# Column tiles for the remainders of a mixture-of-experts kernel's second products, and a smaller descriptor area

## The chip, the cores and the metric

The kernel runs on one core of a Trainium2 chip. The metric is the device time of one execution in microseconds (us), the median of the runs. Lower is better.

## The reference

Attention with a decay over 8 batches of 8 heads, 576 positions and 64 values per head gives 4608 rows of 512 features. Each row goes to the one expert of 8 that has its largest gate logit.

```python
for e in range(E):                      # E = 8, D = 512, F = 1024, N = 4608
    mask = e_idx == e
    h = np.maximum(x[mask] @ w1[e], 0.0)
    ye = h @ w2[e]
    out[mask] = gate_w[mask, None] * eom[mask, e, None] * ye
```

`gate_w` is the softmax weight of the chosen expert, `eom` a sigmoid gate. `h @ w2[e]` is the second product, which the change touches.

## The kernel before

The first part, up to about 356 us, is attention, with the routing of the rows beside it. The second part computes the experts one after the other. Experts 0 and 1 come first with 640 rows each; the other six are ranked by their counts and get the capacities of `CAPS`: 640, 608, 592, 576, 560 and 512 rows. Rows beyond an expert's capacity would go through a loop at the end (`tc.For_i`, line 1255 for the end of a block and line 1323 for the end of the program), which makes no turn with these inputs.

For each expert the rows are gathered from a buffer in DRAM by indirect DMAs on POOL's queue (line 808), 128 at a time, and turned by DMA transposes on SP's queue (`gather_turn`, line 814) into `xT`.

The first products (`up_products`, line 1057) go over 8 chunks `fc` of the hidden features. For each chunk and each of 4 parts of the contraction there are three products (upper by upper, upper by lower and lower by upper half of the operands' split into two 16-bit numbers). The moving operand is `xT`, 512 rows and then the rest of the capacity, and the result stands in `hp` (two buffers for each column piece). ACT takes the positive part into `hh` (line 1066), DVE the remainder of that rounding into `hl` (line 1067); `split_w2` splits the expert's second weights in between, on DVE and POOL in turns (line 1001).

The second products (`down_sum`, lines 1079 to 1085) go over row tiles of 128 rows. A tile is one sum in PSUM: for each of the 8 chunks three matmuls, whose stationary operand is `hh` or `hl` (128 features by 128 rows) and whose moving operand is a chunk of `w2`, 512 columns wide. A capacity that is no multiple of 128 gets a whole last tile; its superfluous rows have indices beyond the output and are not written. `y`, the sum, has two buffers.

After each tile `down_out` (line 1093) evicts `y` on ACT with the row's weight as scale into `ys` (three buffers), and POOL scatters the 128 rows to the output by an indirect DMA (line 1094). In between, the next expert's first weights are split on ACT and POOL (`load_w1`, lines 776 and 777), two chunks after each of the first four tiles.

The order on each engine is that of the code (`manual_schedule`). On PE the sums of an expert's tiles follow each other, and the next expert's first products follow the last tile.

[...]

Of the kernel before, what the change touches and what calls it, by code (L numbers as in the profile page):

```python
# [9 lines left out]
F32 = mybir.dt.float32  # L10
# [5 lines left out]
ALU = mybir.AluOpType  # L16
# [4 lines left out]
P = 128  # L21
B, H, S, D = 8, 8, 576, 64
NT = B * S
DM = H * D
# [48 lines left out]
def attn_moe(tc, *args, **kw):  # L73
    with ExitStack() as ctx:
        _attn_moe(ctx, tc, *args, **kw)


def _attn_moe(ctx, tc, qk, vm, f, wg, w1, w2, out):
    nc = tc.nc
# [685 lines left out]
    NF = FF // P  # L765
    ND = DM // P

    def fetch_w1(pool, we, fc, bufs):
        raw = pool.tile([P, ND, P], F32, name="w1r", bufs=bufs)
        nc.sync.dma_start(raw, we[fc])  # L770
        return raw
# [17 lines left out]
    W2, W2r = [], {}  # L789
# [13 lines left out]
    def rows_x(pool, ids=None):  # L803
        return (pool.tile([P, CT, 2], I32, name="ids") if ids is None else ids,
                pool.tile([P, CT, 2, 2, DM // P // 2, P], F16, name="xT", bufs=1))

    def gather_rows(x, t, known=NT):
        nc.gpsimd.indirect_dma_start(
            out=xg[:, t], out_offset=None, in_=xbuf[0:known],
            in_offset=bass.IndirectOffsetOnAxis(ap=x[0][:, t, 0:1], axis=0),  # L810
            bounds_check=known - 1, oob_is_err=False)

    def gather_turn(x, t):
        nc.sync.dma_start_transpose(x[1][:, t].rearrange("p h j k n -> p (h j k) n"), xg[:, t])
# [174 lines left out]
    m2 = ctx.enter_context(tc.tile_pool(name="m2", bufs=2, reuse_waits="tile"))  # L989
    m1 = ctx.enter_context(tc.tile_pool(name="m1", bufs=1, reuse_waits="tile"))  # L990
    pm = ctx.enter_context(tc.tile_pool(name="pm", bufs=2, space=PSUM, reuse_waits="tile"))
    def fetch_w2(we, fc):
        raw = m2.tile([P, DM], F32, name="w2r", bufs=6)
        nc.sync.dma_start(raw, we[fc])
        return raw

    def split_w2(raw, eng):
        h = m2.tile([P, DM], F16, name="w2h", bufs=8)
        l = m2.tile([P, DM], BF16, name="w2l", bufs=8)
        nc.scalar.copy(out=h, in_=raw)  # L1000
        eng.tensor_tensor(l, raw, h, op=ALU.subtract)  # L1001
        return h, l
# [42 lines left out]
    def hidden():  # L1045
        return m1.tile([P, NF, CAP], F16, name="hh"), m1.tile([P, NF, CAP], F16, name="hl")

    def up_products(w1s, x, cols, fc):
        xT = x[1]
        wh, wl = w1s[fc]  # L1050
        hp = [pm.tile([P, 512], F32, name=f"hp{j}", bufs=2) for j in range(len(cols))]
        for k in range(ND):
            for i, (w, j) in enumerate(((wh, 0), (wh, 1), (wl, 0))):
                for m, (c0, c1) in zip(hp, cols):
                    t0, t1 = c0 // P, c1 // P
                    x = xT[:, t0:t1, k // 2, j, k % 2] if c1 % P == 0 else xT[:, t0, k // 2, j, k % 2, 0:c1 - c0]
                    nc.tensor.matmul(m[:, 0:c1 - c0], w[:, k], x,  # L1057
                                     start=k == 0 and i == 0, stop=k == ND - 1 and i == 2)
        return hp

    def up_split(hp, h, cols, fc):
        hh, hl = h
        for m, (c0, c1) in zip(hp, cols):
            sl = slice(c0, c1)
            m = m[:, 0:c1 - c0]
            nc.scalar.activation(out=hh[:, fc, sl], in_=m, func=AF.Relu)  # L1066
            nc.vector.scalar_tensor_tensor(hl[:, fc, sl], m, 0.0, hh[:, fc, sl],  # L1067
                                           op0=ALU.max, op1=ALU.subtract)

    def up(w1s, x, cols, h=None):  # L1070

        h = h or hidden()
        for fc in range(NF):
            up_split(up_products(w1s, x, cols, fc), h, cols, fc)
        return h

    def down_sum(w2s, h, t):
        hh, hl = h
        y = pm.tile([P, DM], F32, name="y", bufs=2)
        sl = slice(t * P, (t + 1) * P)  # L1080
        for fc in range(NF):
            wh, wl = w2s[fc]
            nc.tensor.matmul(y, hh[:, fc, sl], wh, start=fc == 0, stop=False)  # L1083
            nc.tensor.matmul(y, hh[:, fc, sl], wl, start=False, stop=False)  # L1084
            nc.tensor.matmul(y, hl[:, fc, sl], wh, start=False, stop=fc == NF - 1)  # L1085
        return y
# [3 lines left out]
    def down_out(x, y, t, looped=False):  # L1090
        ids = x[0]
        ys = m2.tile([P, DM], F32, name="ys", bufs=3)
        nc.scalar.activation(out=ys, in_=y, func=AF.Copy, scale=ids[:, t, 1:2].bitcast(F32))  # L1093
        ins = nc.gpsimd.indirect_dma_start(  # L1094
            out=out, out_offset=bass.IndirectOffsetOnAxis(ap=ids[:, t, 0:1], axis=0),
            in_=ys, in_offset=None, bounds_check=NT - 1, oob_is_err=False)
        if not looped:
            for other in written:
                tc.declare_no_dep(ins.ins, other.ins, reason="distinct rows")
            written.append(ins)  # L1100

    def down(w2s, x, h, t0, t1, looped=False):
        for t in range(t0, t1):
            down_out(x, down_sum(w2s, h, t), t, looped)

    def weights(load, we):
        return [load(we, fc) for fc in range(NF)]

    def load_w1(we, fc, raws=None, eng=nc.gpsimd):
        return split_w1(m2, raws[fc] if raws else fetch_w1(m2, we, fc, 8), 8, eng)  # L1110


    x = st["early"]

    with tc.manual_schedule(engines=ENGINES):
# [15 lines left out]
        h = hidden()  # L1131
# [27 lines left out]

        first_splits(0, 4)  # L1160
        down_out(x, down_sum(W2, h, 0), 0)
        for t in range(CT):
            gather_rows(x1, t)
# [6 lines left out]
        W1, W2, x = W1n, [], x1  # L1170
# [20 lines left out]
        ids = m1.tile([P, R, CT, 2], I32, name="idsr")  # L1191
# [12 lines left out]
        def pieces(cap):  # L1204

            return [(0, SM)] + ([(SM, cap)] if cap > SM else [])

        def expert(r):

            cap = CAPS[r]  # L1210
            ei = nc.values_load(rank[0:1, r:r + 1], engines=[mybir.EngineType.SP], min_val=0, max_val=E - 1)
            return dict(cap=cap, ids=ids[:, r],
                        w1=w1[bass.ds(ei, 1)].rearrange("a f p k n -> (a f) p k n"),
                        w2=w2[bass.ds(ei, 1)].rearrange("a f p n -> (a f) p n"))

        e = dict(cap=CAP, w2=w2[1])
        for n in range(len(CAPS) + 1):
            cap = e["cap"]
            cols = pieces(cap) if n else [(0, EARLY), (EARLY, CAP)]
            tiles = -(-cap // P)  # L1220
            nx = expert(n) if n < len(CAPS) else None
            nt = -(-nx["cap"] // P) if nx else 0
            for fc in range(NF):
                up_split(up_products(W1, x, cols, fc), h, cols, fc)
                W2.append(split_w2(W2r[fc], nc.gpsimd if fc % 2 else nc.vector))
                if fc + AHEAD < NF:
                    W2r.append(fetch_w2(e["w2"], fc + AHEAD))
                if nx:
                    if fc == 0:
                        x1 = rows_x(m2, nx["ids"])  # L1230
                    if 2 <= fc < 2 + nt:
                        gather_rows(x1, fc - 2)
                    if fc >= NF - AHEAD:
                        W1r = (W1r if fc > NF - AHEAD else []) + [fetch_w1(m2, nx["w1"], fc - NF + AHEAD, 8)]
            W1n, W2n = [], []
            for t in range(nt):
                gather_turn(x1, t)
            for t in range(tiles):
                y = down_sum(W2, h, t)
                if nx:  # L1240
                    for fc in range(2 * t, min(2 * t + 2, NF)):
                        W1n.append(load_w1(nx["w1"], fc, W1r))
                        if fc + AHEAD < NF:
                            W1r.append(fetch_w1(m2, nx["w1"], fc + AHEAD, 8))
                    if t == 3:
                        W2r = [fetch_w2(nx["w2"], fc) for fc in range(AHEAD)]
                down_out(x, y, t)
                if n == 0 and t == 3:
                    ncum = overflow_slots()
                if n == 2 and t == 0:  # L1250
                    nsl = nc.values_load(ncum, min_val=0, max_val=(NT - min(CAPS)) // P + E)
            if nx:
                e, x, W1, W2 = nx, x1, W1n, W2n

    with tc.For_i(0, nsl, 1) as i:
# [7 lines left out]
        n = pr.tile([P, 512], F32, name="ms", bufs=1)  # L1263
# [8 lines left out]
        x = rows_x(m2)  # L1272
# [7 lines left out]
        h = up(weights(load_w1, w1[bass.ds(ei, 1)].rearrange("a f p k n -> (a f) p k n")), x, [(0, P)])  # L1280
# [46 lines left out]
```

## Time and profile before

| | |
|---|---|
| median of 3 runs | 752.74 us (752.64 to 755.38) |
| profiled execution | 751.45 us, its span 749.8 us |
| PE busy | 721.5 us (96%), 8819 matmuls |
| POOL busy | 456.9 us (61%) |
| DVE, ACT busy | 357.5 us (48%), 339.8 us (45%) |
| mean granted TensorE clock | 0.994 of full speed |

The span runs from the first to the last instruction of the profiled execution. An engine's busy time counts its computing instructions and POOL's DMA instructions; semaphores, branches and drains are not counted. Ends of matmuls are modelled, so the time of one is read from the distance of the starts. `L1084` is line 1084, and `out<-in` names the tiles that an instruction writes and reads.

### The profile page before, as it was taken

Reading aid. Unit: us, or ns where it says so; the run is one execution under the profiler, and the core shown is the slowest. Engines: PE = TensorE matmul, PEld = TensorE weight load, DVE = VectorE, ACT = ScalarE, POOL = GpSimd, SP = SyncE. Lnnn points to the kernel's source line nnn. Section 1 sums busy time; section 2 is a strip of 40 time slices with the busy share of each in tenths; the row PEclk is TensorE's granted clock in tenths of the full one; section 3 lists DMA queues with packets and bytes.
Section 4 is the critical chain, followed back from the end, with each engine's and each line's share of the span. In section 5 each row is a group of like instructions: output and inputs, shape, how many; then the busy total and the mean of one; then the engine's idle time right before and its main releaser. Section 6 shows DMA issues by size and latency. Waiting matters only on the chain. (4 is left out here: it accounts for less than half of the span.)

```text
span 749.8 us, 21552 instructions
## 1 busy us (share of the span) xinstructions
PE 721.5 (96%) x8819; PEld 446.8 (60%) x8842; DVE 357.5 (48%) x837; ACT 339.8 (45%) x765; POOL 456.9 (61%) x513
## 2 busy tenths in 40 slices
PE   4999999999999999999999999999999999999993
PEld 2677777777777777776567545445454454444441
DVE  7667687788788887877314133113022031130210
ACT  4456665567666565654323423324324243243320
POOL 9969698898989898862603544534626436345121
PEclk9999999999999999999999999999999999999997
DMA  5445566666777566265744734825836448256100
GB/s 154 156 127 175 160 169 156 162 166 162 186 176 181 150 168 137 59 145 167 193 108 156 162 125 155 244 75 154 235 121 138 179 136 224 82 155 204 47 29 24
DMA packets 119525, 110.67 MB, mean 148 GB/s; under 512 B 82750, under 2 KB 92158, under 8 KB 119424
## 3 DMA queue, kind: packets, MB, share of 16 engines
q1 hardware_dynamic: 108566, 71.50, 36.8%
q10 hardware_dynamic: 4618, 18.88, 8.5%
q0 software_dynamic: 6240, 18.88, 7.9%
q8 instruction: 70, 1.15, 0.6%
q14 instruction: 31, 0.25, 0.1%
HBM read 72.47 MB, written 19.88 MB: 123 GB/s over the span
## 5 line engine op out<-in xcount | busy, mean ns | idle before, releaser
L428 POOL TENSOR_TENSOR plo<-p 128x512 f16<-128x512 f32 x182 | 191.6, 1069 | 34.7 <-ACT p L426 33.3
L1057 PE MATMUL hp<-xT,w1h 128*128 128x512 f16 (+2 forms) x960 | 174.9, 298 | 0.1
L1067 DVE SCALAR_TENSOR_TENSOR hl<-hp,hh 128x512 f16<-128x512 f32 (+2 forms) x120 | 54.2, 485 | 247.0 <-ACT hh L1066 241.5
L426 ACT ACTIVATE p<-sc 128x512 f32<-128x512 f32 x192 | 111.6, 595 | 70.9 <-PE sc L305 64.5
L331 DVE TENSOR_REDUCE nR<-mx 128x2 f32<-128x1024 f32 (+4 forms) x154 | 121.4, 805 | 46.2 <-PE mx L305 44.5
L305 PE MATMUL sc<-qk 64*128 64x448 f32 (+5 forms) x644 | 128.1, 471 | 0.0
L1085 PE MATMUL y<-w2h,hl 128*128 128x512 f16 x312 | 118.2, 379 | 1.2
L1083 PE MATMUL y<-w2h,hh 128*128 128x512 f16 x312 | 118.2, 379 | 0.0
L1057 PE MATMUL hp<-xT,w1l 128*128 128x512 f16 (+2 forms) x480 | 111.8, 298 | 0.0
L1084 PE MATMUL y<-w2l,hh 128*128 128x512 bf16 x289 | 109.5, 379 | 0.0
L1057 PEld LDWEIGHTS <-w1h 128*128 128x128 f16 x960 | 74.6, 98 | 55.6 <-issue 0.2
L1066 ACT ACTIVATE hh<-hp 128x512 f16<-128x512 f32 (+2 forms) x120 | 47.0, 433 | 118.3 <-PE hp L1057 116.6
L1001 POOL TENSOR_TENSOR w2l<-w2r,w2h 128x512 bf16<-128x512 f32 x28 | 32.3, 1153 | 103.1 <-ACT w2h L1000 103.1
L305 PEld LDWEIGHTS <-pick 64*128 64x128 bf16 (+1 forms) x1152 | 58.3, 96 | 48.7 <-issue 26.3
L1094 POOL DMA_INDIRECT out_dram<-ys,idsr x29 | 29.0, 1001 | 72.9 <-ACT ys L1093 68.7
L1093 ACT ACTIVATE ys<-y,idsr 128x512 f32<-128x512 f32 x29 | 19.9, 688 | 104.6 <-issue 60.1
L499 PE MATMUL av<-Vs,p 128*128 128x65 f16 x640 | 66.0, 193 | 1.3 <-ACT xr L546 1.3
L500 PE MATMUL av<-Vs,p 128*128 128x64 bf16 x640 | 65.8, 195 | 0.6 <-issue 0.6
L501 PE MATMUL av<-Vs,plo 128*128 128x65 f16 x640 | 65.5, 192 | 0.0
L305 PE MATMUL mx<-qk 64*128 64x512 bf16 (+3 forms) x372 | 57.3, 301 | 8.3 <-DMA qk<-in_qk_dram 5.5
L500 PEld LDWEIGHTS <-p 128*128 128x128 bf16 x640 | 59.4, 97 | 1.4 <-issue 1.4
L499 PEld LDWEIGHTS <-p 128*128 128x128 bf16 x640 | 59.2, 97 | 1.3
(219 smaller groups left out, 1397.4 us busy)
## 6 DMA issues: line engine op xcount, KB each, us to landing
qk<-in_qk_dram ACTq DMA_DIRECT2D x31, 576.0 KB
w1r<-in_w_dram SPq DMA_DIRECT2D x64, 256.0 KB
w2r<-in_w_dram SPq DMA_DIRECT2D x64, 256.0 KB
v<-in_vm_dram SPq DMA_DIRECT2D x15, 576.0 KB
xbuf<-x SPq DMA_DIRECT2D x16, 512.0 KB
Eq<-mts SPq DMA_DIRECT2D x64, 0.1 KB
xbuf<-x SPq DMA_DIRECT2D x16, 64.0 KB
xT<-x SPq DMA_TRANSPOSE x62
```

Source lines behind the costliest of these rows:

```text
L305: nc.tensor.matmul(dst(i), w(i), x(i), start=start, stop=stop)
L331: nc.vector.tensor_reduce(o, x, axis=AX.X, op=ALU.max, negate=True)
L426: nc.scalar.activation(out=f32, in_=src, func=AF.Exp, scale=0.125)
L428: eng.tensor_tensor(lo, f32, upper(f32), op=ALU.subtract)
L499: nc.tensor.matmul(dst, ph, vv[:, 0:W], start=kc == 0, stop=False)
L500: nc.tensor.matmul(dst[:, 0:D], ph, vv[:, W:].bitcast(BF16), start=False, stop=False)
L501: nc.tensor.matmul(dst, pl, vv[:, 0:W], start=False, stop=kc == qc)
L1057: nc.tensor.matmul(m[:, 0:c1 - c0], w[:, k], x, start=k == 0 and i == 0, stop=k == ND - 1 and i == 2)
L1067: nc.vector.scalar_tensor_tensor(hl[:, fc, sl], m, 0.0, hh[:, fc, sl], op0=ALU.max, op1=ALU.subtract)
L1083: nc.tensor.matmul(y, hh[:, fc, sl], wh, start=fc == 0, stop=False)
L1084: nc.tensor.matmul(y, hh[:, fc, sl], wl, start=False, stop=False)
L1085: nc.tensor.matmul(y, hl[:, fc, sl], wh, start=False, stop=fc == NF - 1)
```

## The change

The last tile of an expert, if it has at most 96 rows, is no longer computed by `down_sum` and `down_out`, but by `down_narrow`. It takes the first 64 rows as a group of column tiles 64 wide and, if there are more, the next 32 as a group of column tiles 32 wide. In a group of `n` rows, `k = 128 / n` matmuls stand beside each other in the array, each with its own chunk of the contraction; their sums come to lie in different partitions of one PSUM bank, and `narrow_out` adds them on DVE with the row's weight: one operation for the first, one for each further. The scatter then covers 64 or 96 rows. The number of matmuls of a group stays 24, each of 512 columns. The descriptor area is 2048 bytes instead of the default.

```diff
+        put_rows(ys, x, t, looped)
+
+    def put_rows(ys, x, t, looped=False):
         ins = nc.gpsimd.indirect_dma_start(
-            out=out, out_offset=bass.IndirectOffsetOnAxis(ap=ids[:, t, 0:1], axis=0),
+            out=out, out_offset=bass.IndirectOffsetOnAxis(ap=x[0][0:ys.shape[0], t, 0:1], axis=0),
             in_=ys, in_offset=None, bounds_check=NT - 1, oob_is_err=False)
...
+    def narrow_sum(w2s, h, r0, n):
+
+        hh, hl = h
+        y = pm.tile([P, DM], F32, name="y", bufs=2)
+        k = P // n
+        for f0 in range(NF // k):
+            for i in range(3):
+                for j in range(k):
+                    fc = j * (NF // k) + f0
+                    nc.tensor.matmul(y[j * n:(j + 1) * n], (hl if i == 2 else hh)[:, fc, r0:r0 + n],
+                                     w2s[fc][i % 2], start=f0 == i == 0, stop=f0 == NF // k - 1 and i == 2)
+        return y
+
+    def narrow_out(x, t, ys, y, n, p0):
+
+        w = x[0][p0:p0 + n, t, 1:2].bitcast(F32)
+        dst = ys[p0:p0 + n]
+        nc.vector.tensor_scalar(dst, y[0:n], w, None, op0=ALU.mult)
+        for j in range(1, P // n):
+            nc.vector.scalar_tensor_tensor(dst, y[j * n:(j + 1) * n], w, dst, op0=ALU.mult, op1=ALU.add)
+
+    def down_narrow(w2s, x, h, t, rest):
+
+        ys = m2.tile([P, DM], F32, name="ys", bufs=3)
+        for p0, n in ((0, 64), (64, 32)):
+            if p0 < rest:
+                y = narrow_sum(w2s, h, t * P + p0, n)
+                narrow_out(x, t, ys, y, n, p0)
+        put_rows(ys[0:64 if rest <= 64 else 96], x, t)
...
             for t in range(tiles):
-                y = down_sum(W2, h, t)
+                rest = cap - t * P
+                y = down_sum(W2, h, t) if rest > 96 else None
...
-                down_out(x, y, t)
+                if y is None:
+                    down_narrow(W2, x, h, t, rest)
+                else:
+                    down_out(x, y, t)
...
-    nc = _bacc.Bacc("TRN2", target_bir_lowering=False, num_devices=1)
+    nc = _bacc.Bacc("TRN2", target_bir_lowering=False, num_devices=1, dynamic_dma_scratch_size=2048)
```

## Rows read from the trace of the kernel before

**Rows 1.** The page's first part: busy time, share of span, instructions.
```profile
PE 721.5 (96%) x8819; PEld 446.8 (60%) x8842; DVE 357.5 (48%) x837; ACT 339.8 (45%) x765; POOL 456.9 (61%) x513
```
**Rows 2.** Stretches: length, busy us (instructions) by engine, granted clock, DMA share, GB/s.
```profile
521.57:547.47 25.90, 25.74 (x119) 11.73 (x121) 0.85 (x2) 8.43 (x15) 14.27 (x13) 1.00 0.73 198
547.47:571.63 24.16, 24.16 (x193) 12.76 (x192) 8.27 (x18) 9.31 (x22) 9.54 (x9) 1.00 0.38 120
571.63:597.53 25.90, 25.74 (x119) 11.77 (x121) 0.84 (x2) 8.12 (x15) 14.27 (x13) 1.00 0.67 196
...
737.60:749.80 12.20, 0.00 (x0) 0.00 (x0) 0.00 (x0) 0.69 (x1) 0.97 (x1) 0.63 0.04 15
```
**Rows 3.** PE in order of time, capacity 608: fifth tile's and next expert's first matmul.
```profile
542.29 0.38 PE L1083 MATMUL y<-w2h,hh 128*128 128x512 f16 x1
...
547.48 0.67 PE L1057 MATMUL hp<-xT,w1h 128*128 128x512 f16 x4
```
**Rows 4.** PE in order of time, attention, 64 rows by 64 columns of the array.
```profile
100.12 0.41 PE L305 MATMUL mx<-qk 64*64 64x512 bf16 x2
100.34 0.40 PE L305 MATMUL mx<-Ek,Eq 63*64 63x512 f16 x2
100.56 0.22 PE L305 MATMUL mx<-qk 64*64 64x64 bf16 x2
100.59 0.22 PE L305 MATMUL mx<-Ek,Eq 63*64 63x64 f16 x2
100.62 0.22 PE L305 MATMUL mx<-negm,pick 64*64 64x64 bf16 x2
100.77 0.54 PE L305 MATMUL sc<-qk 64*128 64x320 f32 x2
```
**Rows 5.** Weight loads in order of time: corners of 64x64, and a full tile.
```profile
100.34 0.14 PEld L305 LDWEIGHTS <-qk 64*64 64x64 bf16 x2
...
547.04 0.10 PEld L1085 LDWEIGHTS <-hl 128*128 128x128 f16 x1
```
**Rows 6.** DVE, ACT and POOL in order of time after that fifth tile; brackets: idle before.
```profile
551.29 0.84 DVE L1067 SCALAR_TENSOR_TENSOR hl<-hp,hh 128x512 f16<-128x512 f32 x2 [28.07 <-ACT hh L1066]
...
547.73 0.69 ACT L1093 ACTIVATE ys<-y,idsr 128x512 f32<-128x512 f32 x1 [4.49 <-PE y L1085]
...
548.69 0.98 POOL L1094 DMA_INDIRECT out_dram<-ys,idsr  x1 [4.18 <-ACT ys L1093]
555.00 1.15 POOL L1001 TENSOR_TENSOR w2l<-w2r,w2h 128x512 bf16<-128x512 f32 x1 [5.33 <-ACT w2h L1000]
```
**Rows 7.** Groups by line and shape: busy us, mean ns, idle before.
```profile
L1067 DVE SCALAR_TENSOR_TENSOR hl<-hp,hh 128x512 f16<-128x512 f32 x48 | 33.2, 692 | 215.9 <-ACT hh L1066 211.3 <-issue 4.5
```
**Rows 8.** Lines 1315 (start), 1323 and 1255 (end): ns min/median/max, first and last start.
```profile
L1315 POOLq INC_SWDGE_SEM  x1: 27/27/27, 0.2 to 0.2; - x1
L1315 POOLq DRAIN  x1: 184/184/184, 0.4 to 0.4; - x1
...
L1323 POOLq EVENT_SEMAPHORE  x4: 17/17/17, 749.0 to 749.6; - x4
L1323 POOLq DRAIN  x3: 40/103/6452, 742.5 to 749.5; - x3
...
L1255 PEldq EVENT_SEMAPHORE  x13: 51/51/51, 737.6 to 742.5; - x13
L1255 POOLq INC_SWDGE_SEM  x1: 1747/1747/1747, 738.7 to 738.7; - x1
```
**Rows 9.** Issues of DMAs by tile: count, median us from issue to landing.
```profile
xg<-xbuf,idsr POOLq DMA_INDIRECT x29, 3.5
out_dram<-ys,idsr POOLq DMA_INDIRECT x29, 2.7
...
xg<-xbuf,ids POOLq DMA_INDIRECT x8, 6.0
...
xg<-xbuf,idsl POOLq DMA_INDIRECT x2, 4.1
```

## The prediction, made before the changed kernel was run

> **What bounds the kernel now.** The first view to read is the page's busy share [rows 1]: PE is busy 96% of the span, every other engine 61% or less. That average says little of one stage, so the next view is the table of stretches [rows 2], cut at the borders between the first products ("up") and the second products ("down") of the ranked experts. In a down stretch of 25.90 us PE is busy 25.74 us, in an up stretch all of 24.16 us, at the full granted clock, while DVE has 0.85 us of work in a down stretch, ACT 8 and POOL 14. The list in order of time shows the same from close by [rows 3]: the fifth row tile of an expert starts at 542.29 us, its successor, the next expert's first product, at 547.48 us, with no idle time noted on either. So in these stages a microsecond taken from PE is a microsecond of the span. The last row of the table [rows 2] shows another kind of stretch: 12.2 us at the end with no matmul at all. What fills it is in the lists by line of the closing instructions [rows 8]: POOL's one long DRAIN of 6.45 us, from 742.5 us on, and after it, from 749.0 us, the last semaphores. All other engines' waits of the loop's end (line 1255) are over by 742.5 us. The page's chain of waits doesn't show this, as it counts no such instruction as work; the drain still stands alone on the path to the end.
>
> **The change, part by part.** *What is removed.* Of the six ranked experts four have a fifth tile with 96, 80, 64 and 48 rows (capacities 608, 592, 576, 560 less 512); those of 640 and 512 rows keep full tiles. Each fifth tile now costs a whole tile: 24 matmuls of 512 columns in 547.48 - 542.29 = 5.19 us [rows 3], 0.216 us apiece. Four make 20.7 us, all on the path.
>
> *What is added on PE.* A remainder is computed in groups of 64 or 32 rows, a group again with 24 matmuls of 512 columns, but in rounds of 2 (64 columns wide) or 4 (32 wide) that lie side by side in the array. A group of 64 has 12 rounds, one of 32 has 6. Remainders 64 and 48 take one group of 64; 96 and 80 take one of 64 and one of 32. That is 4 x 12 + 2 x 6 = 60 rounds. The trace has no column tile that uses all 128 rows. The nearest are the attention's products in 64x64 corners [rows 4]: two matmuls of 512 columns, each in its own rows and columns, start at 100.12 us, the next two at 100.34 us, the following step at 100.56 us. A round costs 0.22 us, not twice 0.216, and its second member lags 0.03 us (0.41 us for the two, where one takes 0.38 in rows 3). The next nearest is the full tile, where matmuls queue at 0.216 us [rows 3]. So a round of two lies between 0.216 us (all at once) and 0.43 us (in turn), one of four between 0.216 and 0.86 us. I take 0.22: the corners too are separate columns of the array with a separate moving operand, and their loads, of 64 columns, are the kind that the change uses [rows 5].
> Loads: a round needs two or four; two take 0.14 us [rows 5], so one takes 0.11 and its partner the same lag of 0.03. In the corners, as in the full tiles, loads run beside matmuls at work, so I count none, but the lag of the members, 0.03 us a group of 64 and 0.09 us a group of 32. If that cover is gone a round has 0.11 us more.
> A change of tile shape: steps of 64 columns in the corners follow each other at 0.03 us (100.56, 100.59, 100.62), and the step after it, with another shape, came 0.15 us later [rows 4], so a change costs 0.12 us. Remainders with one group change twice, those with two groups three times: 10 x 0.12 = 1.2 us.
> Sum: 4 x (12 x 0.22 + 0.03) + 2 x (6 x 0.22 + 0.09) + 1.2 = 10.7 + 2.8 + 1.2 = 14.7 us in place of 20.7: **6.0 us less**. Ends: 60 x 0.216 = 13.0 us with changes at nothing (7.8 less), and 6 groups x 24 x 0.216 + 1.2 = 32.3 us if all wait in turn (11.6 more).
> [...]
>
> *What moves off PE.* The eviction by ACT (0.69 us, starting 0.25 us after the successor has begun [rows 3, 6]) becomes 2 DVE operations for a group of 64 and 4 for one of 32. Their nearest row is the DVE operation of the same width with a PSUM input, 0.69 us [rows 7]. After the last matmul of a remainder 1.4 or 2.8 us of DVE work follow; in the old tile's times it would end near 547.7 + 2.8 = 550.5 us. DVE is free: it idled 28 us before 551.29 us [rows 6]. Were it later, hl would be late, and PE would miss its buffer hp only two steps, some 6 us, after its start. On POOL the scatter of the remainder waits for it, from 548.7 to some 550.7 us, and POOL's next work comes at 555.00 us [rows 6], so nothing stands behind it. The second group needs the y buffer of the fourth tile, which ACT empties within 1 us of that tile's end, 1.8 us before it is asked for. The weights and the gathered rows of the next expert aren't what PE waits for: no idle time stands before its first product [rows 3], and POOL and ACT have some 11 and 17 us to spare in each down stretch [rows 2]; 1 to 3 us less time for them costs nothing. What is late next is again PE.
>
> *The descriptor area.* It is cut from the constructor's default of 16384 bytes to 2048. It takes part in nothing but POOL's 78 indirect DMAs: 29 + 8 + 2 gathers and as many scatters [rows 9]. At the program's start, before any of them, POOL's DRAIN took 0.184 us, and later ones at its end 0.103 and 0.040; the one that follows the 78 took 6.452 us, though the last semaphore of the data was in by 742.5 us [rows 8]. Another POOL instruction that looks after these DMAs went from 0.027 to 1.747 us [rows 8]. I read that as a cost per DMA whose descriptors are still kept: 6.45 / 78 = 0.083 us. No row shows a smaller area, so the ends are 6.45 us (nothing changes) and 0.10 us (nothing kept). If the large area kept all 78, an eighth of it keeps at least 78 / 8, some 10; the rest must have been given back earlier. Estimate: 10 x 0.083 = 0.8 us, **5.6 us less**, all of it at the end where it hides behind nothing. The giving back, 68 x 0.083 us, falls on POOL's DMAs from the tenth on, about 0.8 us per expert against the slack above. A POOL that waits for space meets DMAs ten places back, 25 us or more ago among the experts, that landed after 2.7 to 3.5 us in the median [rows 9]: no wait.
> [...]
>
> **Sum.** 6.0 + 5.6 = 11.6 us less. The profiled execution, 751.45 us with its span of 749.8, would become 739.9 us; it lies 1.3 us under the median of the runs, 752.74 us, from which the forecast is **741.1 us**.
>
> **Rivals.** *The drain doesn't depend on the area* (a fixed price, or one per DMA ever issued): only PE's 6.0 us remain, 746.7 us. For it: no row has another area. Against it: the three short drains and the other instruction's growth.
> *Loads are not covered in column tiles*: a round takes 0.22 + 0.11 us, 60 rounds and the changes 60 x 0.33 + 1.2 = 21.0 us, so nothing is gained on PE; the drain gives 752.7 + 0.3 - 5.6 = 747.4 us.
> *Column tiles run in turn* (the slower side): where two streams through the same 128 rows can't run at once, every narrow matmul takes its 0.216 us, six groups cost 32.3 us, and 752.7 + 11.6 - 5.6 = 758.7 us. The corners don't exclude it, as their rows differ too. It decides from a mean round of (20.7 + 5.6 - 1.2) / 60 = 0.42 us on.
> *Neither part works* (loads uncovered, drain as before): 753 us.
>
> **How the numbers follow.** Forecast 0.60, fixed drain 0.10, loads uncovered 0.12, in turn 0.10, neither 0.05; 0.03 is left for a mixture on the slower side. The forecast's best ends (7.8 and 6.35) give 738.6 us; upwards 747.5 takes in the second and third cases, together 0.82. A measurement can tell about 0.5%, 3.8 us, from no change: faster 0.82 (the first three), same 0.06, slower 0.12.
>
> **What would show it.** After, the four fifth tiles should take 2.9 us (one group) and 4.4 us (two) from their first matmul to the next expert's first, with rounds 0.22 us apart and no idle time on PE behind them; rounds of 0.33 or 0.43 us point to the third and fourth cases. POOL's long DRAIN should be near 1 us, and its DMA instructions still about 1 us. The forecast is wrong if PE idles at the next expert's start for W1, xT or a buffer, or if the drain keeps its 6.45 us.

## The result, and the profile after

| | before | after |
|---|---|---|
| median of 4 runs | 752.69 us (752.23 to 755.38) | 741.84 us (741.30 to 742.90) |
| ratio, 95% interval | | 0.9846 [0.9826, 0.9867] |
| profiled execution, its span | 751.45, 749.8 us | 742.90, 741.2 us |

The change makes the kernel 10.9 us faster, where 11.6 were forecast (741.1 us). The sizes of the two parts are to be read from the stretches and from POOL's closing DRAIN; several terms of the sum were off, and they nearly cancel.

The first part of the page of after answers [rows 1]: PE's busy time fell by 2.9 us only, while DVE took over 12.5 us. The whole kernel's busy time is no measure of the gain here. From the first matmul of the experts' second products on it fell by 6.3 us (379.97 to 373.71); ahead of it, where the change does nothing, it was 3.3 us more (341.54 to 344.88), as after's execution was slower early on (see the last section). The matmuls are more (8871 instead of 8819), as a remainder of two groups has 48 instead of 24.
```profile
PE 718.6 (97%) x8871; PEld 444.3 (60%) x8890; DVE 370.0 (50%) x853; ACT 336.6 (45%) x761; POOL 455.9 (62%) x513
```
Stretches of after, with the columns of [rows 2]: the down stretches of the capacities 608, 592, 576 and 560, and the end without matmuls.
```profile
524.02:548.96 24.94, 24.84 (x145) 11.13 (x145) 2.06 (x4) 8.43 (x15) 14.26 (x13) 1.00 0.77 205
573.13:598.06 24.93, 24.82 (x144) 11.13 (x145) 2.04 (x4) 8.09 (x15) 14.26 (x13) 1.00 0.71 204
621.59:645.12 23.53, 23.42 (x121) 10.59 (x121) 0.82 (x2) 8.21 (x15) 14.25 (x13) 1.00 0.72 205
668.26:691.79 23.53, 23.42 (x121) 10.57 (x121) 0.81 (x2) 8.06 (x15) 14.24 (x13) 1.00 0.63 191
733.40:741.20 7.80, 0.00 (x1) 0.00 (x0) 0.00 (x0) 0.69 (x1) 0.97 (x1) 0.65 0.09 28
```
Each of the four took 25.90 us before. Two fell by 0.96 us (remainders with two groups), two by 2.37 us (one group): 6.7 us in all, where the sum had 6.0. The granted clock is 1.00 in them as before; the only other level on record in the two traces is 0.50, from 740.79 us on in before and from 735.79 us on in after, when the matmuls are over. The end fell from 12.20 to 7.80 us.

PE of after in order of time around the remainder of capacity 608, as [rows 3]; x2 and x4 are matmuls side by side that the view joins.
```profile
544.52 0.38 PE L1085 MATMUL y<-w2h,hl 128*128 128x512 f16 x1
544.84 0.41 PE L1114 MATMUL y<-w2h,hh 128*64 128x512 f16 x2
545.08 0.38 PE L1114 MATMUL y<-w2l,hh 128*64 128x512 bf16 x2
545.29 0.38 PE L1114 MATMUL y<-w2h,hl 128*64 128x512 f16 x2
...
547.23 0.38 PE L1114 MATMUL y<-w2h,hl 128*64 128x512 f16 x2
547.54 0.40 PE L1114 MATMUL y<-w2h,hh 128*32 128x512 f16 x4
547.77 0.39 PE L1114 MATMUL y<-w2l,hh 128*32 128x512 bf16 x4
...
548.63 0.39 PE L1114 MATMUL y<-w2h,hl 128*32 128x512 f16 x4
548.96 0.64 PE L1057 MATMUL hp<-xT,w1h 128*128 128x512 f16 x3
```
From 545.08 to 547.23 us lie 10 rounds of 0.215 us, and from 547.77 to 548.63 us 4 of 0.215 us: two or four matmuls of 512 columns in the time of one, though all of them use the same 128 rows of the array. A change of shape shows as 0.31 us between two starts (547.23 to 547.54), 0.09 us more than a round, and another 0.01 to 0.02 us in the first round after it.

The weight loads of after in order of time, in the same remainder, as [rows 5].
```profile
547.02 0.11 PEld L1114 LDWEIGHTS <-hl 128*64 128x64 f16 x2
547.54 0.12 PEld L1114 LDWEIGHTS <-hh 128*32 128x32 f16 x8 [0.41 <-issue]
547.77 0.11 PEld L1114 LDWEIGHTS <-hl 128*32 128x32 f16 x4
```
The loads of a round take 0.11 us together and lie inside the rounds of 0.215 us.

DVE and POOL of after in order of time behind that remainder, as [rows 6].
```profile
547.72 0.74 DVE L1122 TENSOR_SCALAR ys<-y,idsr 64x512 f32<-64x512 f32 x1 [22.05 <-PE y L1114]
548.50 0.75 DVE L1124 SCALAR_TENSOR_TENSOR ys<-y,idsr,ys 64x512 f32<-64x512 f32 x1
549.28 0.74 DVE L1122 TENSOR_SCALAR ys<-y,idsr 32x512 f32<-32x512 f32 x1
550.06 2.32 DVE L1124 SCALAR_TENSOR_TENSOR ys<-y,idsr,ys 32x512 f32<-32x512 f32 x3
552.78 0.84 DVE L1067 SCALAR_TENSOR_TENSOR hl<-hp,hh 128x512 f16<-128x512 f32 x2 [0.40 <-ACT hh L1066]
```
```profile
552.66 0.94 POOL L1097 DMA_INDIRECT out_dram<-ys,idsr  x1 [5.71 <-DVE ys L1124]
556.49 1.15 POOL L1001 TENSOR_TENSOR w2l<-w2r,w2h 128x512 bf16<-128x512 f32 x1 [2.88 <-ACT w2h L1000]
```
The cover held. hl starts 552.78 - 548.96 = 3.82 us after the next expert's first matmul, as before (551.29 - 547.48 = 3.81 us, [rows 3, 6]), and POOL's next split 7.53 us after it (before: 7.52 us). But DVE had only 0.40 us to spare.

Closing instructions of after by line: minimum, median and longest in ns, first and last start, as [rows 8].
```profile
L1292 PEldq EVENT_SEMAPHORE  x13: 51/51/51, 733.4 to 739.0; - x13
L1292 POOLq INC_SWDGE_SEM  x1: 487/487/487, 734.5 to 734.5; - x1
...
L1360 POOLq DRAIN  x3: 40/103/1307, 739.1 to 740.9; - x3
```
The long DRAIN fell from 6452 to 1307 ns, 5.15 us less (forecast: 5.6). The other instruction, INC_SWDGE_SEM, fell with it, from 1747 to 487 ns.

Last, the way from the last scatter to that DRAIN. After, it took 739.1 - 734.45 = 4.65 us:
```profile
734.45 0.97 POOL L1097 DMA_INDIRECT out_dram<-ys,idsr  x1 [4.26 <-POOLq L1292]
```
and before 742.5 - 738.64 = 3.86 us ([rows 8], and this row of before):
```profile
738.64 0.97 POOL L1094 DMA_INDIRECT out_dram<-ys,idsr  x1 [4.21 <-POOLq L1255]
```
So 0.8 us came back at the end. The sum of the three is -6.68 - 5.15 + 0.8 = -11.0 us, and the medians differ by 10.9. The spans of the two profiled executions differ by 8.55 us only, because after's was 2.3 us behind already at the first matmul of the experts' second products (358.68 us against 356.41), long before the first narrow tile; the last section returns to that.

### The profile page after: what moved, and what is told of

Its sections match the earlier page's. It is cut to its first block, busy times and chain, and to the rows that moved or that the text cites. A ratio compares the mean times of both kernels' runs of the same rounds, so it can differ in the third digit from the quotient of the medians.

```text
span 741.2 us, 21637 instructions
## 1 busy us (share of the span) xinstructions
PE 718.6 (97%) x8871; PEld 444.3 (60%) x8890; DVE 370.0 (50%) x853; ACT 336.6 (45%) x761; POOL 455.9 (62%) x513
## 5 line engine op out<-in xcount | busy, mean ns | idle before, releaser
L1085 PE MATMUL y<-w2h,hl 128*128 128x512 f16 x280 | 106.1, 379 | 1.0
L1083 PE MATMUL y<-w2h,hh 128*128 128x512 f16 x280 | 106.1, 379 | 0.0
L1084 PE MATMUL y<-w2l,hh 128*128 128x512 bf16 x261 | 98.9, 379 | 0.0
L501 PEld LDWEIGHTS <-plo 128*128 128x128 f16 x640 | 59.4, 99 | 0.0
```

What stands on the lines that cost most here:

```text
L501: nc.tensor.matmul(dst, pl, vv[:, 0:W], start=False, stop=kc == qc)
```

## The experiments

### Each part alone

`area_only` is the kernel before with the smaller area.
```diff
-    nc = _bacc.Bacc("TRN2", target_bir_lowering=False, num_devices=1)
+    nc = _bacc.Bacc("TRN2", target_bir_lowering=False, num_devices=1, dynamic_dma_scratch_size=2048)
```


> The kernel before with the small descriptor area alone. Theory (POOL's closing DRAIN costs a fixed 0.18 us and 0.080 us for each indirect DMA whose descriptors are still kept; the line through 6.452 us with 78 kept and 1.307 us after the change gives 14 kept): DRAIN near 1.3 us, the time 5.1 us below before, 747.5 us; POOL's DMA instructions a little longer from the fifteenth on, PE as before. Rival (the DRAIN got shorter because the narrow tiles' scatters are shorter or earlier, not by the area): DRAIN 6.45 us, 752.7 us.

Measured: 748.91 us (748.04 to 751.14) beside 754.97 of before in that session, ratio 0.9922 [0.9896, 0.9947]. Its closing DRAIN, in the list by line:
```profile
L1323 POOLq DRAIN  x3: 40/103/735, 745.8 to 747.1; - x3
```
The price of the DRAIN depends on the area, but 0.735 us is neither the 1.3 us that the theory wanted nor the 1.307 us of the change at the same 2048 bytes. So neither the area nor the 78 DMAs alone set what is kept.

`tiles_only` is the changed kernel with the default area.
```diff
-    nc = _bacc.Bacc("TRN2", target_bir_lowering=False, num_devices=1, dynamic_dma_scratch_size=2048)
+    nc = _bacc.Bacc("TRN2", target_bir_lowering=False, num_devices=1)
```


> The change with the descriptor area left at its default. Theory: the down stretches of the four ranked experts stay at 24.94, 24.94, 23.53 and 23.52 us instead of 25.90, which is 6.7 us together, and the DRAIN is back at 6.4 us: 746.1 us. Rival (the two parts help each other, for example the tiles are only fed in time with POOL relieved): less than 5 us below before, with idle time on PE behind a narrow tile.

Measured: 747.29 us (745.81 to 750.09), ratio 0.9904 [0.9876, 0.9931]. One down stretch, and the closing instructions by line:
```profile
522.34:547.27 24.93, 24.93 (x146) 11.10 (x145) 2.06 (x4) 8.42 (x15) 14.24 (x13) 1.00 0.78 205
```
```profile
L1292 POOLq INC_SWDGE_SEM  x1: 1747/1747/1747, 732.8 to 732.8; - x1
...
L1360 POOLq DRAIN  x3: 40/103/6452, 736.8 to 743.8; - x3
```
The four down stretches are those of the change to 0.01 us, and the DRAIN is that of before. So the area does nothing to the tiles. The tiles do touch the DRAIN, though only where the area is small: it takes 0.735 us without them and 1.307 us with them. By the medians the parts gain 6.1 and 7.7 us, by the rows 5.0 (the DRAIN and the way to it) and 6.4; the intervals, 4.0 to 7.9 and 5.2 to 9.4 us, take that in. The product 0.9922 x 0.9904 = 0.9827 lies at the edge of the interval of the change, so the sum is better read from the rows. The rivals "fixed drain" and "neither" fall, each by its own run.

### Column tiles in turn

`one_by_one` gives PE the same matmuls in another order: all of one column tile, then all of the next.
```diff
-        for f0 in range(NF // k):
-            for i in range(3):
-                for j in range(k):
+        for j in range(k):
+            for f0 in range(NF // k):
+                for i in range(3):
```


> The changed kernel with the loop over the column tiles outermost in a group, so that neighbours in PE's queue belong to the same column tile. Theory (tiles run beside each other only where neighbours in the queue belong to different ones): each of the six groups takes 24 x 0.216 = 5.2 us instead of 2.6 (64 wide) or 1.3 (32 wide), 4 x 2.6 + 2 x 3.9 = 18 us more than the changed kernel, near 760 us, slower than before. Rival (PE picks matmuls of free column tiles out of its queue): 742 us as with the change.

Measured, in a single execution: 751.91 us. The down stretches are 28.02, 28.02, 25.28 and 25.28 us, 9.7 us more than in the change: neither the 18 us of a strict order nor nothing. PE in order of time in the group of 64 rows:
```profile
545.70 0.38 PE L1114 MATMUL y<-w2l,hh 128*64 128x512 bf16 x1
545.92 0.38 PE L1114 MATMUL y<-w2h,hl 128*64 128x512 f16 x1
545.92 0.59 PE L1114 MATMUL y<-w2h,hh 128*64 128x512 f16 x2
546.16 0.56 PE L1114 MATMUL y<-w2l,hh 128*64 128x512 bf16 x2
546.38 0.56 PE L1114 MATMUL y<-w2h,hl 128*64 128x512 f16 x2
546.60 0.38 PE L1114 MATMUL y<-w2h,hh 128*64 128x512 f16 x1
```
Up to 545.92 us one matmul starts every 0.215 us. Then the second column tile's first matmul starts beside the first tile's ninth, while the tenth to twelfth, which stand before it in the program, are still to come; they start in the next three rounds, each beside one of the second tile. The rows don't name the column tile; it follows from the order of the operands, which repeats with each chunk (w2h,hh, then w2l,hh, then w2h,hl). So a tile's end overlaps the next one's beginning by four rounds. That gives 24 - 4 = 20 rounds for a group of 64 (12 in the change) and, with three such borders, 24 - 12 = 12 rounds for one of 32 (6 in the change). A remainder of two groups then has 14 rounds more, 14 x 0.2155 = 3.0 us, and one of one group 8, 1.7 us; measured were 28.02 - 24.94 = 3.08 and 25.28 - 23.53 = 1.75 us. The theory that wanted 18 us, in which matmuls start in the program's order without exception, falls, and so does the one that wanted nothing: PE reaches ahead, but only by three matmuls.

### Only groups of 32

`groups_32` takes the 64 rows of the first group as two groups of 32. The rounds on PE stay as many (6 + 6 instead of 12), DVE gets 8 operations instead of 2 for these rows.
```diff
-        for p0, n in ((0, 64), (64, 32)):
+        for p0, n in ((0, 32), (32, 32), (64, 32)):
```


> The changed kernel with all remainders in groups of 32 rows: two groups for 64 and 48 rows, three for 96 and 80. The rounds on PE stay 60, two changes of tile shape fall away (0.2 us less), and DVE has 8 or 12 operations of 0.69 us per remainder instead of 2 or 6. Theory (PE's cover holds only as far as y's two buffers): the third group waits for the first one's four DVE operations, which end some 1.3 + 2.8 = 4.1 us after the remainder's start where it is asked for after 2.7 us; 1.4 us of idle time on PE in each of the two remainders with three groups, none before the next expert's products: 741.8 + 2.8 - 0.2 = 744.4 us. Rival (DVE is late for the next expert's hl as well): idle time also on PE within the next first products, 2 us or more for each remainder, 750 us or more. Rival (DVE keeps up): 741.6 us.

Measured: 748.03 us (747.25 to 748.72) beside 754.97, ratio 0.9908 [0.9877, 0.9939]. Its stretches say how much of the tiles' gain is gone: the down stretches are 26.95, 26.95, 23.52 and 23.52 us, 4.0 us more than in the change, and the first products behind two of them take 0.7 us more, 4.7 of 6.7 us in all. PE in order of time, at the border of the second and the third group of capacity 608:
```profile
546.84 0.39 PE L1114 MATMUL y<-w2h,hl 128*32 128x512 f16 x4
549.18 0.40 PE L1114 MATMUL y<-w2h,hh 128*32 128x512 f16 x4 [1.95 <-DVE ys L1124]
```
and DVE of that kernel:
```profile
546.05 0.74 DVE L1122 TENSOR_SCALAR ys<-y,idsr 32x512 f32<-32x512 f32 x1 [20.76 <-PE y L1114]
546.82 2.31 DVE L1124 SCALAR_TENSOR_TENSOR ys<-y,idsr,ys 32x512 f32<-32x512 f32 x3
```
PE makes a group of 32 in 1.3 us, DVE empties its y in 3.1 us, and y has two buffers: the third group starts 0.05 us after DVE has left the first. That costs 1.95 us in each of the two remainders with three groups. Where there are only two groups, the down stretch is that of the change (23.52 us), but the DVE work runs on into the next expert, and behind one of them PE waits 0.51 us for hl:
```profile
701.36 0.59 PE L1057 MATMUL hp<-xT,w1h 128*128 128x512 f16 x2 [0.51 <-DVE hl L1067]
```
This wait comes 701.36 - 695.49 = 5.9 us after that expert's first matmul, at the place where the prediction put it (two steps, some 6 us). So the choice of 64 before 32 matters, and it matters on DVE, not on PE. The mechanism was the expected one, the size was not: 1.95 us of idle time in place of 1.4, and the wait for hl of the first rival beside it, though not behind every remainder.

### The size of the area

Five kernels differ from the change in one number, the area: `area_512`, `area_1024`, `area_3072`, `area_4096` and `area_8192`. `change_again` is the change itself once more (2048).
```diff
-    nc = _bacc.Bacc("TRN2", target_bir_lowering=False, num_devices=1, dynamic_dma_scratch_size=2048)
+    nc = _bacc.Bacc("TRN2", target_bir_lowering=False, num_devices=1, dynamic_dma_scratch_size=512)
```
`area_512` and `area_4096` were run first, to see whether the DRAIN goes with the area.

> The changed kernel with an area of 512 bytes, a quarter of the change's. Theory (a fixed 0.18 us and 0.080 us for each DMA kept, 3 or 4 kept): DRAIN near 0.45 us, 0.85 us below the changed kernel, near 741.0 us. Rival (POOL now waits for space, since the DMA three places back was issued only 4 us ago where five gathers follow each other at 1.3 us, and gathers land after 3.5 to 6 us): POOL's DMA instructions or the waits before them grow to several us, gathers come late, and PE idles before an expert's first products: 742 us or more, up to 750.

> The changed kernel with an area of 4096 bytes, twice the change's. Theory (0.18 us and 0.080 us for each DMA kept, twice as many kept, 28): DRAIN near 2.4 us, 1.1 us above the changed kernel, near 742.9 us. Rival (the DRAIN's length has a step, not a slope: short as soon as the area has been used more than once): 1.3 us, 741.8 us. Rival (it counts all DMAs ever issued as soon as the area holds more than a few): 6.45 us, 747 us.

Measured: 741.26 us, ratio 0.9839 [0.9811, 0.9866] and 741.92 us, ratio 0.9838 [0.9813, 0.9864]. Their DRAINs by line, first with 512 bytes, then with 4096:
```profile
L1292 POOLq INC_SWDGE_SEM  x1: 247/247/247, 732.8 to 732.8; - x1
...
L1360 POOLq DRAIN  x3: 40/103/327, 737.2 to 738.3; - x3
```
```profile
L1292 POOLq INC_SWDGE_SEM  x1: 467/467/467, 734.6 to 734.6; - x1
...
L1360 POOLq DRAIN  x3: 40/103/1225, 739.1 to 740.8; - x3
```
A DRAIN that grows with the area would be 2.4 us with 4096 bytes; it is a little shorter than with 2048. That theory, which is also the prediction's (an eighth of the area keeps an eighth of the DMAs), fell. The next one: each DMA whose descriptors are still kept costs 0.0815 us on top of 0.083 us; descriptors are given back only when a new DMA finds no space, and then those of all DMAs but the last seven. What is kept at the end then depends on where in this cycle the last DMA falls, and must be worked out DMA by DMA; where fewer than eight DMAs find room (512 and 1024 bytes), the oldest goes for each new one. Three more areas were run on that theory.

> The changed kernel once more, beside the next ones on the same chip: its DRAIN 1.31 us as before, 0.985 of the kernel before.

> The changed kernel with an area of 1024 bytes. New theory from the five DRAINs seen so far (0.327, 0.735, 1.225, 1.307 and 6.452 us): the DRAIN takes 0.083 us and 0.0815 us for each DMA whose descriptors are still kept, and POOL gives descriptors back only when a new DMA finds no space, then all but the last seven DMAs. At 1024 bytes (half of the 14 DMAs of 2048) seven are kept at any time: DRAIN 0.65 us, 0.65 us below the change. POOL gives one back at each DMA. Rival (each DMA then waits for its seventh predecessor): gathers later by microseconds, idle time on PE, slower than the change.

> The changed kernel with an area of 3072 bytes, between 2048 (DRAIN 1.307 us) and 4096 (1.225 us). New theory (all but the last seven DMAs are given back when space runs out; 21 full DMAs fit, so that happens at the DMAs 22, 36, 50 and 64, and from then on, with two shorter scatters, 22 stay): DRAIN 0.083 + 22 x 0.0815 = 1.88 us, longer than with either neighbour. Rival (the DRAIN grows with the area or has a step): between 1.2 and 1.3 us.

> The changed kernel with an area of 8192 bytes. New theory (56 full DMAs fit; with the shorter scatters space runs out once, at DMA 58, and all but seven go; 28 are kept at the end): DRAIN 0.083 + 28 x 0.0815 = 2.36 us. Rival (half of the default, so half of its kept DMAs or the share of the area): 3.2 us; rival (what fits is kept): 56 to 58, 4.7 us.

Measured: `change_again` 743.12 us, ratio 0.9859 [0.9838, 0.9881]; `area_1024` 741.98 us, 0.9852 [0.9822, 0.9881]; `area_3072` 743.66 and `area_8192` 743.46 us in a single execution each. By these times no area from 512 to 8192 bytes can be told from another; the DRAINs can. The table has all areas in the order of the DRAIN; "kept" is the whole number that the two formulas want.

| kernel | area, bytes | kept | DRAIN, ns | 83 + 81.5 x kept | INC_SWDGE_SEM, ns | 187 + 20 x kept |
|---|---|---|---|---|---|---|
| area_512 | 512 | 3 | 327 | 328 | 247 | 247 |
| area_1024 | 1024 | 7 | 653 | 654 | 327 | 327 |
| area_only | 2048 | 8 | 735 | 735 | 347 | 347 |
| area_4096 | 4096 | 14 | 1225 | 1224 | 467 | 467 |
| the change | 2048 | 15 | 1307 | 1306 | 487 | 487 |
| area_3072 | 3072 | 22 | 1878 | 1876 | 627 | 627 |
| area_8192 | 8192 | 28 | 2368 | 2365 | 747 | 747 |
| before, tiles_only | 16384 | 78 | 6452 | 6440 | 1747 | 1747 |

The expectations for 3072 bytes (1.88 us, longer than with 4096) and 8192 bytes (2.36 us) were met to 0.01 us. The second formula was found afterwards and wasn't fitted to the DRAINs: one whole number in each row serves both instructions, and for the default area it is 78, all indirect DMAs of the program. Worked out DMA by DMA, with 144 bytes for a DMA of 128 rows and three quarters or half of that for the scatters of 96 and 64 rows, the theory gives all eight numbers of the table; with six or eight in place of seven, or with 136 or 160 bytes, it does not. The 144 is an estimate from these DRAINs: of the whole numbers from 60 to 299 only 143 and 144 give all eight. In the change space runs out at the DMAs 15, 22, 29 and so on, the last time at 71, so that the seven then kept and the eight DMAs from 71 to 78 are there at the end. In `area_only`, without the shorter scatters, the 78th itself finds no space, which leaves seven and itself. What isn't shown is why seven, nor the giving back itself: the traces have the lengths of the DRAINs and the delays below, not the descriptors.

Where the theory has descriptors given back, POOL starts a DMA later. With the change and with the default area, the same scatter (the 71st of the 78 DMAs):
```profile
680.16 1.02 POOL L1097 DMA_INDIRECT out_dram<-ys,idsr  x1 [2.17 <-ACT w1h L776]
```
```profile
678.15 1.02 POOL L1097 DMA_INDIRECT out_dram<-ys,idsr  x1 [1.85 <-ACT ys L1093]
```
POOL was idle 2.17 instead of 1.85 us before it. These 0.3 us for one DMA in seven lie in POOL's slack. They come where the theory has them: with starts counted from the first matmul of the second products, the DMAs 15, 22, 43, 64 and 71 of the change are 0.3 us later than in `tiles_only` (29, 36, 50 and 57, all gathers, are not), in `area_3072` the 22nd and 64th by 0.4 us, and in `area_4096` the 72nd, not the 71st, by 0.5 us. With 512 bytes, where by the theory three DMAs find room, the DMAs 7 to 12, between 364 and 375 us, come up to 3.5 us late: the 10th, a gather, starts 372.24 - 363.37 = 8.87 us after the 6th, where before has 5.4 us. The median of that kernel, 741.26 us, shows nothing of it.

## Why the prediction was right, point by point

*What bounds the kernel.* Right. Time taken from PE in the down stretches left the span one for one (25.90 to 24.94 and 23.53 us, no idle time at the next expert's first matmul), and the end shrank with the DRAIN.

*Rounds.* Taken at 0.22 us by the corners of [rows 4], measured 0.2155 us, the full tile's own pitch: 60 x 0.0045 = 0.3 us too much.

*Lag of the members.* Counted at 0.03 us a group of 64 and 0.09 us a group of 32, 0.3 us in all. Within a round of the change the members start 3 to 4 ns apart, and in the pitch of the rounds nothing of it is left. This term should not have been in the sum: the corners of [rows 4] had a lag of 0.03 us too, and their rounds still followed each other at 0.22 us.

*Changes of shape.* Taken at 0.12 us each from the step in [rows 4]. What remains of the measured time is 20.7 - 6.68 - 60 x 0.2155 = 1.1 us for ten: 0.11 us each. The three terms together are the 0.7 us by which the tiles gained more than 6.0. A remainder with one group took 2.7 us from its first matmul to the next expert's (2.9 forecast), one with two groups 548.96 - 544.84 = 4.1 us (4.4).

*Work moved to DVE.* Right that it is hidden, too optimistic by how much. Its six operations take 552.38 - 547.72 = 4.66 us, 0.78 us apiece with the gap between two, where 0.69 was taken; they end 3.4 us after the next expert's first matmul instead of 3.0, and hl stands 0.40 us behind. `groups_32` shows what lies beyond: with six operations more for 64 rows y's buffers and then hl hold PE up.

*The scatter and POOL.* Right: the scatter starts 3.7 us after the next expert's first matmul instead of the forecast 3.2, and POOL's next work is not delayed.

*The descriptor area.* The price per DMA, 0.083 us, was right (0.0815 and a constant). The number kept was mis-sized: "some 10", as an eighth of the 78, and it is 15. The step that failed is the proportion: by the theory that gives all eight DRAINs nothing is given back until the area is full, so the 78 said nothing of how many the large area could hold. Nor does the giving back cost 0.083 us at each DMA, as forecast, but 0.3 us at one in seven. By the same theory 14 DMAs of 128 rows find room in 2048 bytes (2048 / 144 = 14.2). That isn't what is kept at the end, which is 15 in the change, and 8 in `area_only` with the same 2048 bytes.

*What was missed.* That the last scatter would be over later. With the default area the DRAIN starts 3.9 us (before) and 736.8 - 732.77 = 4.0 us (`tiles_only`) after the last scatter, with 2048 bytes 4.6 us (`area_only`: 745.8 - 741.21) and 4.65 us (the change), with 512 bytes 4.5 us. It takes back 0.6 to 0.8 us of the DRAIN's gain. The trace shows where the time goes: into the transfer. The last of its sixteen semaphore increments comes 2.61 us after the scatter's start in before and 2.85 us in `tiles_only`, but 3.37 us in `area_only`, 3.41 us in the change and 3.06 to 3.68 us in all other kernels with a smaller area, and the DRAIN starts 1.2 us after it in every one. INC_SWDGE_SEM, which starts 0.07 us after the scatter in before and in the change, is 1.3 us shorter with the small area (487 instead of 1747 ns), so it isn't what the end waits for, but it may have a part in it: POOL comes to its next branch that much sooner, and a packet of 8 KB of the queue that the page calls q14 instruction starts 1.58 to 1.76 us after the scatter's start in `area_only` and the change, while the scatter's packets are under way (1.54 to 3.07 us after its start in the change), and 2.94 to 2.96 us after it with the default area, when they are over (1.54 to 2.28 us in before). That this packet holds the scatter up is a conjecture, as the trace doesn't say which DMA engine carries what. That the delay goes with the small area is shown, why it does stays open.

*Rivals.* "Loads uncovered" would have shown rounds of 0.33 us, "in turn" of 0.43 us (64 wide) and 0.86 us (32 wide); there were 0.2155 us. "Fixed drain" and "neither" fell with `area_only` and `tiles_only`. Of the net, 0.7 us more from the tiles, 0.45 less from the DRAIN and 0.8 back at the last scatter make 10.9 to 11.0 us out of the forecast 11.6. That the sum came so close is in part luck: the tiles' error and the other two have opposite signs.

## What to carry to other kernels

A remainder of 64 or 32 rows was worth column tiles here (0.96 or 2.37 us each), as the members of a round follow each other in the program (with the tiles in turn, `one_by_one`, the down stretches took 9.7 us more) and DVE has time for the extra additions: count the operations that empty PSUM against its buffers before choosing the narrower tile (in `groups_32` PE idled 1.95 us for them). Look at a program's last microseconds by line, control instructions too, as the busy shares don't show them: here 12.20 us without a matmul, 6.45 of them in one DRAIN. That DRAIN became 5.15 us shorter with an area an eighth as large, at the price of 0.3 us of POOL's slack at one DMA in seven and of 0.8 us at the last scatter. A cost per item that is read well from one row still needs the number of items, and a number that comes from a cycle doesn't scale with the size of the thing that fills (the table has 15 kept with 2048 bytes, 22 with 3072 and 14 with 4096).

## What was not expected of the hardware

- PE starts a matmul of another column tile before up to three matmuls that stand ahead of it in the program (`one_by_one`), as at 545.92 us there, so even a poor order lost only 9.7 of 18 us.
- Four column tiles of 32, fed with four separate moving operands of 128 rows, keep a round of 0.2155 us, like one full tile.
- POOL's closing DRAIN fits 0.083 us and whole steps of 0.0815 us to within 12 ns: 0.327 to 2.368 us with areas of 512 to 8192 bytes, which the theory reads as 3 to 28 indirect DMAs still kept, and 6.452 us with the default area, which it reads as all 78.
- Executions differ early on. In before, matmuls of 512 columns came down from 0.63 to 0.40 us by 13.8 us after the start, in after only between 19.9 and 22.3 us. PE in order of time, first of before, then of after, then of `tiles_only`:
```profile
13.15 0.63 PE L305 MATMUL mx<-Ek,Eq 63*64 63x512 f16 x2
...
13.84 0.40 PE L305 MATMUL av<-qk 64*128 64x512 bf16 x2
```
```profile
19.91 0.63 PE L305 MATMUL av<-Ek,Eq 63*128 63x512 f16 x2
...
22.31 0.43 PE L305 MATMUL sc<-Eq,Ek 64*128 64x512 f16 x2
```
```profile
18.60 0.62 PE L305 MATMUL mx<-Ek,Eq 63*64 63x512 f16 x2
...
21.64 0.38 PE L305 MATMUL sc<-Eq,Ek 64*128 64x512 f16 x2
```
This goes with the granted clock. Its first record in the trace, at 1.00, begins at 13.75 us in before and at 22.41 us in after; the views count the time ahead of the first record as 1.00. In `tiles_only` the level is on record on both sides: the stretch from 17.80 to 21.10 us has a granted clock of 0.50, the one from 21.20 us on 1.00, and the rows of 0.62 and 0.38 us stand one in each. Why the clock rose later in one execution than in another stays open.

Over the profiles of this study the first matmul of the second products lies anywhere between 356.4 and 359.0 us, with no order by kernel, but mostly with one by the clock: 356.4 us in before, 356.8 in `area_512` and 358.0 in `one_by_one`, where 1.00 came on record at 13.7 to 14.3 us and stayed; 357.2 in `tiles_only`, 357.5 in `area_1024` and 358.6 in `change_again`, where it came then too but was lost until 21.2 to 21.6 us; 358.3 to 359.0 us in the six others, where it came at 22.3 to 23.9 us. What put `one_by_one` and `change_again` over a microsecond behind their neighbours isn't known. Single spans can't be compared to better than 2.6 us without taking that out; stretches and medians can.
